# One input load held back behind TensorE's dummies, two head steps exchanged, one dummy pair less

## The chip, the cores and the metric

The kernel runs on one core of a Trainium2 chip. The metric is the device time of one execution in microseconds (us); lower is better.

## The reference

```python
x = A_x                                                # (1, 2048, 640) bf16
g = sigmoid((x * gate_w).sum(-1, keepdims=True))
# A: linear attention, 32 heads of 20
q, k, v = split(x @ wqkv)                              # wqkv (640, 1920)
pq, pk = q @ w_phi[h], k @ w_phi[h]                    # per head, 20 x 20
phi_q = concat(softmax(pq), softmax(-pq)); phi_k = concat(softmax(pk), softmax(-pk))
kv, z = phi_k^T v, sum_s phi_k
a = ((phi_q kv) / (phi_q z + 1e-6)) @ wo
# B: gated FFN, width 1728
b = (silu(x @ w_gate) * (x @ w_up)) @ w_down
return g * a + (1 - g) * b                             # bf16
```

## The kernel before

The 2048 tokens are cut into 16 tiles of 128 (and into 4 blocks of 512 for the FFN); the 640 columns of x into 5 chunks of 128. All work of all five engines is written as one list of steps. Two strings hold it: `LOADS` (L33), the transfers into the chip, and `ORDER` (L38), the compute steps. L759 goes through both and calls a function per word; every engine then has its instructions in that order. A tracker adds the semaphore waits that the reads and writes need. A DMA has a semaphore of its own; TensorE, ScalarE, VectorE and POOL have one each, which counts their tracked steps.

**Loads.** `LOADS` begins `x0 w0 x1 w1 x2 w2 x3 w3 w4 f0 h k0 k1 t4`. `x0` to `x3` (`load_x`, L369) bring the first four token tiles, 128 x 640, as they are, into `xs`. `w0` to `w4` (`load_wv`) bring the v columns of wqkv in chunks of 128 rows, into `wvg`. Two queues issue them: SP (SyncE) takes x0, w0, w1, w2, w3, and ScalarE takes x1, x2, x3, w4 (L361, L362). Ahead of x1 ScalarE's queue has the load of gate_w (`gwr`), and behind w4 the load of w_phi (`h`, tile `wph`), which waits for w3. Then follow on SP's queue the first FFN weights (`f0`), the transposed chunks of the k weights (`k`, tile `wT`), the token tiles 4 to 15 transposed by DMA (`t`), the q weights (`q`) and the rest.

**The head of the compute.** Words of `ORDER`:

- `H` (`warm`, L470): a dummy pair, two 128-column matmuls of constant ones, whose result nobody reads. The pair counts as one on TensorE's semaphore.
- `G`: gate_w is transposed into a column of `wvg`.
- `X0` to `X3` (`xpose`, L457): TensorE transposes the five chunks of a token tile (L308), VectorE copies them into `xT`; for tiles 0 to 2 the first chunk is copied apart from the other four.
- `U t.c` (`vpart`, L498): the two matmuls (320 and 321 columns, L296) of token tile t with chunk c of `wvg`. Five such parts make the v of a tile; then ScalarE copies it out. A tile's PSUM pair is held from its first part to its last.
- `V t`: the same for a later tile at once.

Before, the head runs `H0 ... H6 G H7 H8 X0 H9 H10 U0.0 X1 H11 U1.0 U0.1 X2 ...`.

**The rest.** `M` and `R` multiply w_phi into the k and q weights, with masked blocks of w_phi (`wbd`) that `Y` makes. `K`, `S`, `P` make phi_k, `E` adds up kv in PSUM banks 6 and 7. `N` (`kv_end`, L744) ends this: it has a loop of `NPEW` waits of TensorE on its own semaphore for the value 1, and then calls `kv_finish`, in which VectorE reads kv and z out of PSUM. `Z` transposes z (`zh`). Then come the q tiles (`Q`, `A`, `B`, `C`, `c`), the FFN (`F`), the attention output (`O`) and the down projection with the store (`D`).

PSUM is used as four pairs of banks. `next_pair` gives the pair used longest ago that isn't held; `H`, `G`, `X`, the first `U` of a tile and most other steps take one, so that the number and the order of the head's steps decide which pair a later step gets. Between `I` and `N` the fourth pair is left to kv.

Of the kernel before, what the change touches and what calls it, by code (L numbers as in the profile page):

```python
# [16 lines left out]
NV = 6  # L17
NWARM = 2
NWAIT = 6
NPEW = 32  # L20
FP = 120 * NCH
FK = FP + 8
ACTF = mybir.ActivationFunctionType
# [12 lines left out]
"""  # L36

ORDER = """  # L38
H0 H1 H2 H3 H4 H5 H6 G H7 H8 X0 H9 H10 U0.0 X1 H11 U1.0 U0.1 X2 U1.1 U2.0 U0.2 U1.2 U2.1
X3 U2.2 U0.3 U1.3 U2.3 U0.4 U1.4 U2.4 V3 Y F0.1 M1 i3 M0 F0.0 M2 V4 M3 M4 K0 K1 I S0 V6 V5 S1 P0  # L40
K3 K2 P1 E0 V9 K4 E1 S3 V7 P3 K5 S2 V8 V10 S4 P2 P4 E2 R0 E3 K6 S5 P5 S6 i4 E4 V14 K7 K8 P6 V15 S7
R2 E5 K9 S8 P7 R1 E6 K10 S9 V12 P8 E7 P9 K11 S10 P10 F0.2 R3 F1.2 E8 E9 K12 E10 S11 S12 K14 S14
# [11 lines left out]
class _Tracker:  # L54
# [90 lines left out]
    def run(self, eng, fn, reads=(), writes=(), dma=False):  # L145
        rkeys = list(dict.fromkeys(k for a in reads for k in self.keys_of(a)))
        wkeys = list(dict.fromkeys(k for a in writes for k in self.keys_of(a)))
        need = {}

        def req(ev, raw):  # L150
            if ev is None:
                return
            s, v = ev
            if s == eng and not dma and (eng == "pe" or not raw):
                return
            if v > need.get(s, 0):
                need[s] = v

        for k in rkeys:
            for kk in self._conflicts(k):  # L160
                req(self.lastw[kk], True)
                if k[0] == "psum":
                    for s, v in self.readers[kk].items():
                        req((s, v), False)
        for k in wkeys:
            for kk in self._conflicts(k):
                req(self.lastw[kk], True)
                for s, v in self.readers[kk].items():
                    req((s, v), False)
        self._wait(eng, need)  # L170
        ins = fn()
        if dma:
            sn = "d%d" % self.ndma
            self.ndma += 1
            self._add_sem(sn)
            inc = 16
        else:
            sn, inc = eng, 1
        ins.then_inc(self.sem[sn], inc)
        self.cnt[sn] += inc  # L180
        v = self.cnt[sn]
        snap = dict(self.known[eng])
        if not dma:
            snap[sn] = max(snap.get(sn, 0), v)
        self.evknow.setdefault(sn, {})[v] = snap
        ev = (sn, v)
        for k in wkeys:
            self.lastw[k] = ev
            self.readers[k] = {}
        for k in rkeys:  # L190
            r = self.readers[k]
            if r.get(sn, 0) < v:
                r[sn] = v
        return ev


def _build(nc, A_x, A_wqkv, A_w_phi, A_wo, B_x, B_w_gate, B_w_up, B_w_down, gate_w, out):
    tr = _Tracker(nc)
    pe, act, dve, pool, sp = nc.tensor, nc.scalar, nc.vector, nc.gpsimd, nc.sync
# [144 lines left out]
    def dma(e, dst, src, transpose=False):  # L344
        eo = tr.eng[e]

        def fn():
            if transpose:
                return eo.dma_start_transpose(dst, src)
            return eo.dma_start(dst, src)  # L350
        rd = [src] if src.tensor.name in tr.base else []
        wr = [dst] if dst.tensor.name in tr.base else []
        return run(e, fn, rd, wr, dma=True)
# [13 lines left out]
        return dma(e, dst, A_wqkv[c * P:(c + 1) * P, c0:c0 + D])  # L367

    def load_x(t):  # L369
        dma(XQ[t], xs[:, t, :], x2[t * P:(t + 1) * P, :])  # L370

    def load_xt(t):
# [27 lines left out]
    H0 = [0, 6, 12, 19, 25]  # L400
    H1 = [7, 13, 20, 26, 32]
# [342 lines left out]
    def kv_end():  # L744
        for _ in range(NPEW):
            pe.wait_ge(tr.sem["pe"], 1)
        kv_finish()
        ring["n"] = 4

    ops = {  # L750
        "H": lambda i: warm(), "i": fills, "X": xpose, "G": gcol, "U": vpart, "V": vtile,
        "M": lambda m: premult(1, m), "R": lambda m: premult(0, m),
        "K": ktile, "S": knorm, "P": kmul, "p": lambda t: kmul(t, "dve"), "E": kvtile, "x": load_x, "t": load_xt, "w": load_wv, "h": load_phi, "k": lambda m: load_wt(1, m), "q": lambda m: load_wt(0, m),
        "f": lambda i: load_ffn(FCUT[i], FCUT[i + 1]), "L": load_late_weights, "T": tail_weights, "J": gates,
        "Y": w_blocks, "I": kv_begin, "N": kv_end, "Z": z_row,
# [50 lines left out]
```

The softmax here doesn't subtract the row's maximum and nothing guards it: scores larger than these inputs give would overflow.

## Time and profile before

| what | value |
|---|---|
| median of 5 runs | 289.34 us (288.52 to 290.21) |
| the profiled execution's own time | 290.64 us |
| its span, first to last instruction | 289.4 us |
| TensorE (PE) busy, share of the span | 285.8 us, 99% |
| ScalarE (ACT) | 151.9 us, 52% |
| VectorE (DVE) | 163.5 us, 57% |
| POOL | 159.9 us, 55% |
| HBM read and written | 9.29 MB and 2.62 MB, 41 GB/s over the span |

PE is TensorE's matmuls, PEld its weight loads, which run beside them. SPq and ACTq are the instructions by which SyncE and ScalarE issue a DMA. The chain follows the work that ended last back to its beginning, at each step to what released it. A wait is idle time of an engine, put down to what came last. Spans on POOL are rough, and the ends of matmuls are modelled: their starts are the surer reading.

### The profile page before, as it was taken

The page shows a single profiled execution, that of the slowest core. Times are in us where ns is not written, and L with a number is a line of the kernel's source. Part 1 is how long each engine was busy: PE and PEld are TensorE (multiplying, and loading weights), DVE is VectorE, ACT ScalarE, POOL GpSimd, SP SyncE. Part 2 cuts the span into 40 slices and gives each one's busy share as a digit, 9 for nine tenths or more (in the row PEclk, how much of TensorE's full clock was granted, in tenths as well). Part 3 has the DMA queues.
Part 4 walks back from the last instruction along what each step waited for, and adds up shares of the span by engine and source line. Part 5 has one row for each costly group of instructions (what it writes and reads, how often), then busy time and mean ns, then how long its engine had stood idle before and what let it go on. Part 6 is the DMA issues. An engine that isn't in the chain of part 4 may idle for free.

```text
span 289.4 us, 4960 instructions
## 1 busy us (share of the span) xinstructions
PE 285.8 (99%) x1973; PEld 175.5 (61%) x1973; DVE 163.5 (57%) x243; ACT 151.9 (52%) x252; POOL 159.9 (55%) x125
## 2 busy tenths in 40 slices
PE   7999999999999999999999999999999999999997
PEld 6667777575644455557775546675554446656776
DVE  2245857587369978769992375980317899100000
ACT  0567768766685565584344763224676552234112
POOL 8275899979645798845633347450653658601000
DMA  7976797000010496402282102052020005210101
GB/s 220 194 119 129 108 280 274 3 0 3 0 49 0 70 329 124 83 17 47 53 144 73 28 1 50 2 120 70 2 50 0 2 2 116 58 45 0 49 23 48
DMA packets 48944, 21.62 MB, mean 75 GB/s; under 512 B 39384, under 2 KB 48792, under 8 KB 48920
## 3 DMA queue, kind: packets, MB, share of 16 engines
q1 hardware_dynamic: 47534, 20.59, 30.8%
q10 hardware_dynamic: 1386, 0.71, 0.9%
q8 instruction: 16, 0.26, 0.4%
q14 instruction: 8, 0.07, 0.1%
HBM read 9.29 MB, written 2.62 MB: 41 GB/s over the span
## 4 chain that ended last, share of the span: by engine, by line
PE 98%; DMA 1%; SPq 0%; DVE 0%; issue 0%
PE ps L296 97%; DMA wvg<-in_A_wqkv_dram 1%; PE ps L308 0%; SPq L350 0%; DVE osb L732 0%; PE ps L477 0%
## 5 line engine op out<-in xcount | busy, mean ns | idle before, releaser
L324 POOL TENSOR_TENSOR hT<-hT,us 128x512 bf16<-128x512 bf16 (+1 forms) x56 | 65.1, 1174 | 66.9 <-DVE hT L328 47.0
L328 DVE SCALAR_TENSOR_TENSOR hT<-hT,ps 128x512 bf16<-128x512 bf16 (+1 forms) x56 | 37.3, 682 | 68.6 <-ACT hT L314 55.0
L296 PE MATMUL ps<-xT,wg 128*128 128x512 bf16 x260 | 64.6, 379 | 0.0
L296 PE MATMUL ps<-xT,wu 128*128 128x512 bf16 x260 | 64.6, 379 | 0.0
L296 PE MATMUL ps<-wd,hT 128*128 128x320 bf16 (+2 forms) x462 | 63.9, 295 | 0.0
L324 POOL TENSOR_TENSOR ph<-eq,qc 128x1320 bf16<-128x1320 bf16 x16 | 42.4, 2647 | 25.6 <-DVE qc L637 20.8
L296 PEld LDWEIGHTS ps<-wd,hT 128*128 128x128 bf16 x462 | 44.5, 98 | 17.4
L296 PE MATMUL ps<-wqk,xT 128*128 128x320 bf16 x320 | 47.7, 299 | 0.0
L314 ACT ACTIVATE hT<-ps 128x512 bf16<-128x512 f32 (+2 forms) x60 | 35.7, 596 | 16.7 <-PE ps L296 16.5
L296 PEld LDWEIGHTS ps<-xT,wu 128*128 128x128 bf16 x260 | 25.4, 98 | 30.7
L314 ACT ACTIVATE us<-ps 128x512 bf16<-128x512 f32 (+1 forms) x56 | 33.5, 598 | 19.2 <-PE ps L296 18.2
L314 ACT ACTIVATE osb<-ps,omg 128x640 bf16<-128x640 f32 (+2 forms) x17 | 12.9, 758 | 55.7 <-PE ps L296 55.7
L296 PEld LDWEIGHTS ps<-xT,wg 128*128 128x128 bf16 x260 | 25.0, 98 | 27.8 <-ACT oT L314 0.8
L324 POOL TENSOR_TENSOR ekr<-ekr,krec 128x1280 bf16<-128x1280 bf16 x16 | 37.4, 2358 | 5.8 <-DVE krec L338 5.8
L296 PEld LDWEIGHTS ps<-wqk,xT 128*128 128x128 bf16 x320 | 30.5, 98 | 13.1 <-issue 0.4
L314 ACT ACTIVATE eq<-ps 128x640 bf16<-128x640 f32 x32 | 22.4, 704 | 20.9 <-POOL ph L324 10.7
L335 DVE TENSOR_REDUCE ksum<-ekr 128x64 f32<-128x1280 bf16 x16 | 23.5, 1470 | 11.8 <-ACT ekr L314 11.8
L314 ACT ACTIVATE ekr<-ps 128x640 bf16<-128x640 f32 x32 | 22.3, 704 | 8.7 <-PE ps L296 8.2
L296 PE MATMUL ps<-wvg,xT 128*128 128x320 bf16 (+1 forms) x160 | 25.6, 309 | 0.8 <-DMA wvg<-in_A_wqkv_dram 0.8
L335 DVE TENSOR_REDUCE qz<-eq 128x64 f32<-128x1280 bf16 x16 | 23.7, 1478 | 2.6 <-ACT eq L314 2.6
L296 PE MATMUL ps<-wog,oT 128*128 128x320 bf16 (+2 forms) x165 | 24.7, 294 | 0.0
L335 DVE TENSOR_REDUCE qw<-ez 128x64 f32<-128x1280 bf16 x16 | 23.6, 1476 | 0.0
(73 smaller groups left out, 191.1 us busy)
## 6 DMA issues: line engine op xcount, KB each, us to landing
out_dram<-osb SPq DMA_DIRECT2D x15, 160.0 KB, 2.0
wd<-in_B_w_down_dram SPq DMA_DIRECT2D x1, 2080.0 KB, 10.9
wg<-in_B_w_gate_dram SPq DMA_DIRECT2D x1, 1040.0 KB, 10.3
wu<-in_B_w_up_dram SPq DMA_DIRECT2D x1, 1040.0 KB, 12.3
wg<-in_B_w_gate_dram SPq DMA_DIRECT2D x1, 800.0 KB, 5.8
wu<-in_B_w_up_dram SPq DMA_DIRECT2D x1, 800.0 KB, 8.0
wog<-in_A_wo_dram SPq DMA_DIRECT2D x2, 375.0 KB, 7.3
wvg<-in_A_wqkv_dram SPq DMA_DIRECT2D x4, 160.0 KB, 3.9
```

The lines of the kernel that those rows point to most:

```text
L296: last = pe.matmul(o, lhsT=l, rhs=r, start=st, stop=sp_, skip_group_check=sk)
L314: return run("act", lambda: act.activation(o, i, func, scale=scale), rd, [o])
L324: return run(e, lambda: eo.tensor_tensor(o, a, b, op), [a, b], [o])
L328: return run("dve", lambda: dve.scalar_tensor_tensor(out=o, in0=a, scalar=s, in1=b, op0=op0, op1=op1), rd, [o])
L335: return run("dve", lambda: dve.tensor_reduce(o, i, AX.X, ALU.add), [i], [o])
```

## The change

Three edits and a constant.

- `load_x(1)` makes ScalarE wait for the value 4 of TensorE's semaphore before it issues the load of x1. At that point of the program only dummy pairs count, so this is the end of H3. The queue is in order: x2, x3, w4 and wph are issued after x1.
- In `ORDER` the dummy pair H10 stands behind U0.0 instead of in front of it; H11, which stood between X1 and the v parts, is gone; and U0.1 comes ahead of U1.0.
- `NPEW` goes from 32 to 40.

```diff
-NPEW = 32
+NPEW = 40
...
 ORDER = """
-H0 H1 H2 H3 H4 H5 H6 G H7 H8 X0 H9 H10 U0.0 X1 H11 U1.0 U0.1 X2 U1.1 U2.0 U0.2 U1.2 U2.1
+H0 H1 H2 H3 H4 H5 H6 G H7 H8 X0 H9 U0.0 H10 X1 U0.1 U1.0 X2 U1.1 U2.0 U0.2 U1.2 U2.1
...
     def load_x(t):
+        if t == 1:
+            act.wait_ge(tr.sem["pe"], 4)
         dma(XQ[t], xs[:, t, :], x2[t * P:(t + 1) * P, :])
```

## The prediction

> **What bounds the kernel now.** I read the page first (busy shares, then the chain that ended last), then the chain in order of time, and then only the first 10 us, because everything else is closed. The page says:
>
> ```profile
> PE 285.8 (99%) x1973; PEld 175.5 (61%) x1973; DVE 163.5 (57%) x243; ACT 151.9 (52%) x252; POOL 159.9 (55%) x125
> PE 98%; DMA 1%; SPq 0%; DVE 0%; issue 0%
> ```
>
> TensorE is busy 99% of the span and is 98% of the chain. The chain in order of time shows where the other 2% lies:
>
> ```profile
> 1.27 3.64 DMA wvg<-in_A_wqkv_dram
> 4.91 0.14 issue
> 5.04 0.69 PE ps L296 x2
> 5.74 0.53 PE ps L308 x5
> 6.27 0.21 PE ps L477 x2
> 6.48 1.07 PE ps L296 x4
> 7.55 0.53 PE ps L308 x5
> ```
>
> From 5.04 us on the chain never leaves TensorE. So the end moves only with the moment at which the dense stretch starts, and with the rate of its first matmuls. It starts when the first wv rows (w0) land, at 1.27 + 3.64 = 4.91. The waits say the same, and the table of 0.4 us stretches shows TensorE empty while the DMA engines are full:
>
> ```profile
> PE ps L296 <- DMA wvg<-in_A_wqkv_dram: 0.8, 1, 0.8
> 4.20:4.60 0.40, 0.01 (x1) 0.00 (x0) 0.04 (x1) 0.00 (x0) 0.40 (x2) 1.00 0.90 314
> 4.60:5.00 0.40, 0.00 (x0) 0.00 (x0) 0.00 (x0) 0.00 (x0) 0.40 (x2) 1.00 1.05 365
> ```
>
> (Columns: stretch, PE, PEld, DVE, ACT, POOL busy, clock, DMA share, GB/s.) What competes is in the timeline of the two issuing queues:
>
> ```profile
> 0.80 0.40 SPq L350 DMA_DIRECT2D xs<-in_A_x_dram  x1
> 1.27 1.85 SPq L350 DMA_DIRECT2D wvg<-in_A_wqkv_dram  x4
> 1.40 1.32 ACTq L350 DMA_DIRECT2D xs<-in_A_x_dram  x3
> 2.75 0.45 ACTq L350 DMA_DIRECT2D wvg<-in_A_wqkv_dram  x1
> 7.74 0.42 ACTq L350 DMA_DIRECT2D wph<-in_A_w_phi_dram  x1
> ```
>
> The issue times and landings of the single transfers in the trace give: x0 3.02, w0 4.91, x1 (issued 1.40) 5.09, w1 5.41, x2 5.81, w2 6.24, x3 7.30, w3 7.72, w4 8.07.
>
> Single matmuls give the rate. Starts of 320-column matmuls are 267 ns apart until 8.7 us and 138 ns apart after 8.9; the 128-column ones are 107 ns apart early and 55 late. The page's granted clock says 1.00 throughout and doesn't show this.
>
> [...]ten of w0's sixteen completions were in by 3.73, the last, [...]came at 4.91.[...]
>
> **The change, part by part.**
>
> *The wait.* TensorE's semaphore counts 1 per dummy pair and reaches 4 at 1.87 in the trace. A DMA that carries a wait left 0.02 us after its event (wph at 7.74, after w3 landed at 7.72), so x1 is issued at 1.89 instead of 1.40: +0.49. Behind it on ScalarE's queue stand x2, x3, w4 (each +0.49: 2.29, 2.76, 3.24), and wph, which waits for w3 of SP's queue and stays at 7.74. ScalarE's table load (8.25) and first copy (11.55) stay too. SP's and POOL's queues have no wait added.
>
> *Who wants these loads.* x1 landed at 5.09 and was used at 5.53, so it is tight. x2 (5.81, used 7.35), x3 (7.30, used 9.70) and w4 (8.07, used 11.08) keep 1.0 us or more after +0.49. Every later load up to 40 us has 2.9 us or more of slack in the trace, except wph, whose products are done at 13.29 and used at 15.22.
>
> *w0.* x1's first packets were on the DMA engines at 2.92, and should now be there at about 3.41, when SP's queue had begun 234 row packets, against 256 in x0 and w0 together, even with x1 beside them. So w0 should land sooner. Bounds: 3.73 (ten engines of sixteen) and 4.91 (unchanged, if one slow engine held it, not x1). I take 4.1. The issue step was 0.14, so the first matmuls with w0 (U0.0) start at 4.24, end at 4.24 + 2 x 0.267 = 4.77, and the dummy pair H10 behind them ends at 4.98.
>
> *x1.* Bounds: 5.09 (the bandwidth that w0 no longer shares pays for the delay) and 5.58 (+0.49 in full); beyond that, 6.2 if it meets a slow packet (single packets in this stretch took up to 0.68 us). I take 5.3, so X1 starts at 5.35: TensorE idles 0.37 there.
>
> *Order and dummies.* From X1 to X2 the trace of before has 5 transposes (0.53), H11 (0.21) and four matmuls (1.07): 5.53 + 1.81 = 7.35. After, H11 is gone and U0.1 covers VectorE's copy of x1 (0.23) that H11 covered: 5.35 + 0.53 + 1.07 = 6.95. The same count with w0 unchanged: 5.04 + 0.53 + 0.21 + 0.53 + 1.07 = 7.39, so the pair removed saves nothing by itself (H10 now stands behind w0 in its place, and before w0 TensorE idles anyway). U0.1 needs w1, at 5.41 before and wanted at 5.88: no wait. X2 is 0.39 earlier; all matmuls behind it are the same, and PSUM pairs are only renamed (the seven reuses whose predecessor differs all have their reader done over 1 us before).
>
> *At which rate.* If the clock switches at 8.8 as before, the 0.39 us gained are half-rate time, worth 0.20; if the switch moves along, 0.39. I take 0.3.
>
> *The eight waits more at L745.* They pass at once. 32 of them are 16 sequencer instructions, 0.106 us apart from 76.95 to 78.57, while the array works off queued matmuls until 79.38. Twenty end at 79.0, before the transpose of zh that follows them loads its weights at 79.24: nothing, with 0.2 us of cover left. If that cover is gone, the price is at most 4 x 0.106 = 0.42; below nothing I see no mechanism. They also replace the four TensorE instructions of the dummy pair[...].
>
> **Sum.** -0.3 us. The profiled execution took 290.64 (span 289.4 and 1.24 around), 1.30 above the median of 289.34; its own time would be 290.3, the median 289.0. A change within 0.5% (1.45 us) is about what a measurement of this kernel can't tell from none.
>
> **Rivals.**
>
> *An earlier clock.* The idle of 0.84 us before w0 shrinks[...] For it: the five times spread over 1.69 us[...]. Against it: a gap of about 0.4 us in front of X1 stays, and one before w0.
>
> *Nothing.* One slow engine, not x1, held w0: X2 at 7.39, time 289.4. For it: one packet at 4.05 took 0.61 us.
>
> *x1 becomes the bound (slower).* In front of X1, TensorE waits for x1 instead of w0. The point is X1 at 7.35 - 1.60 = 5.74, x1 landing at 5.70. At 6.2 the loss is 0.5 us: 289.8.[...] For it: x1, x2 and x3 all leave 0.49 later on a saturated DMA. Against it: the same bytes in the same total time, and w0 served first.
>
> *The wait does nothing.* It can't: the fourth pair ends 0.46 us after x1's old issue.
>
> **How the numbers follow.** Forecast, a small gain (0 to 1.4 us): 0.56. Earlier clock, past 1.45 us: 0.12. Nothing: 0.12. x1 late by less than 1.45 us: 0.12[...]. So faster 0.12, same 0.80, slower 0.08. The likeliest time is 289.0. Its head runs from 288.7 (x1 at 5.09: X2 0.60 earlier) to 289.8 (x1 at 6.2); a median of few runs that spread 1.69 adds some 0.5 each side, and part of the earlier clock belongs in: 287.6 to 290.2.
>
> **What would show it.** Right: x1's issue at 1.9; w0 landing before 4.5; the wait in front of TensorE's first wv matmuls shorter than 0.8 and a new one of TensorE for x1 in front of its transposes; X2 near 6.95; no idle later, none near 79 us. Wrong: w0 still at 4.9, x1 after 5.7[...].

## The result, and the profile after

The changed kernel takes 290.55 us (median of 36 executions, 288.87 to 291.77); the kernel before, beside it, 289.23 (71 executions). The ratio is 1.0033, 95% interval 1.0021 to 1.0046: slower by about a third of a percent, where 289.0 us was forecast and 287.6 to 290.2 stated. (One slow run, 293.43 us in a_nowait below, is left out of its ratio; medians and counts include it.)

The medians hide the shape. Half of the executions after (18 of 36) lie above 290.7 us; before it was 8 of 71, and 14 of 227 over all runs of the kernel before in this study. The change made a rare outcome common. The line at 290.7 is a rough one: the execution profiled before, at 290.64, belongs to the upper group by its trace, as shown below. Drawn at 290.5, the counts are again 18 of 36 after, and 10 of 71 before.

The profiled execution after is one of the other half: its own time is 289.37, its span 288.1, less than the 289.4 of the execution profiled before. One profile against one profile points the wrong way here.

The chain in order of time, after (start, length, what):

```profile
0.84 1.24 PE ps L479 x10
2.08 0.17 ACTq L350
2.25 0.03 issue
2.28 4.43 DMA xs<-in_A_x_dram
6.71 0.05 issue
6.76 0.45 PE ps L308 x5
7.21 1.37 PE ps L296 x10
8.58 0.28 PE ps L308 x5
8.86 69.40 PE ps L296 x640
```

The transfer in the chain is no longer w0 but x2, issued by ScalarE's queue at 2.28 and landed at 6.71; and the chain reaches back through that queue to TensorE's dummies, which release it. The last two lines are X3 and what follows it. The timeline of ScalarE's issues shows the hold (x1 leaves at 1.89 instead of 1.40), and TensorE's timeline where it waits:

```profile
1.89 1.32 ACTq L350 DMA_DIRECT2D xs<-in_A_x_dram  x3
3.24 0.45 ACTq L350 DMA_DIRECT2D wvg<-in_A_wqkv_dram  x1
4.08 0.69 PE L296 MATMUL ps<-wvg,xT 128*128 128x320 bf16 x2 [0.19 <-DMA wvg<-in_A_wqkv_dram]
4.57 0.42 PE L479 MATMUL ps<-const-bfloat16-1.0 128*128 128x128 bf16 x2
5.22 0.45 PE L308 MATMUL ps<-ident,xs 128*128 128x128 bf16 x5 [0.23 <-DMA xs<-in_A_x_dram]
5.51 0.71 PE L296 MATMUL ps<-wvg,xT 128*128 128x320 bf16 x4
6.76 0.45 PE L308 MATMUL ps<-ident,xs 128*128 128x128 bf16 x5 [0.55 <-DMA xs<-in_A_x_dram]
7.05 1.53 PE L296 MATMUL ps<-wvg,xT 128*128 128x320 bf16 x10
8.42 0.44 PE L308 MATMUL ps<-ident,xs 128*128 128x128 bf16 x5
```

w0 is early and its wait is down to 0.19 us. Two new waits stand in its place, in front of X1 (5.22) and of X2 (6.76). The bracket counts from the modelled end of the matmul before; from start to start the gaps are 0.54 and 0.84 us. The rate is the other thing to read. The granted clock in the tables is 1.00 in both profiles, so "half" and "full" clock stand here for the spacing of the matmuls' starts alone: 267 and 138 ns with 320 columns, 107 and 55 with 128. The five transposes of X1 take 0.71 us at half rate (a_npew32 and d_gap below); here they take 0.45. In this execution the dummy pair at 4.57 is still 107 ns apart, and from 5.28 the transposes are 56 apart: the clock was full at 5.3 us, while before it was half until 8.7. That is why this profile is short.

One number puts everything else aside. The span less the start of X3 is 279.7 us after (288.12 - 8.42) and before (289.40 - 9.70), and, within 0.06 us, in all profiles of this study but one (c_pe2, with one stall of 0.34 at 13.5 us). So in the profiled executions the differences arise before X3, from two things: when the loads of the head land (x1, x2 and the first chunks of w), and when the clock goes full.

### The profile page after: what moved, and what is told of

Its sections match the earlier page's. It is cut to its first block, busy times and chain, and to the rows that moved or that the text cites. A ratio compares the mean times of both kernels' runs of the same rounds, so it can differ in the third digit from the quotient of the medians.

```text
span 288.1 us, 4960 instructions
## 1 busy us (share of the span) xinstructions
PE 284.4 (99%) x1971; PEld 173.9 (60%) x1971; DVE 163.5 (57%) x243; ACT 151.8 (53%) x252; POOL 159.8 (55%) x125
## 4 chain that ended last, share of the span: by engine, by line
PE 97%; DMA 2%; DVE 0%; ACTq 0%; issue 0%
PE ps L296 97%; DMA xs<-in_A_x_dram 2%; PE ps L479 0%; PE ps L308 0%; DVE osb L734 0%; ACTq L350 0%
## 5 line engine op out<-in xcount | busy, mean ns | idle before, releaser
L296 PE MATMUL ps<-wvg,xT 128*128 128x320 bf16 (+1 forms) x160 | 24.5, 301 | 0.2 <-DMA wvg<-in_A_wqkv_dram 0.2
## 6 DMA issues: line engine op xcount, KB each, us to landing
wg<-in_B_w_gate_dram SPq DMA_DIRECT2D x1, 1040.0 KB, 10.1
```

The costliest lines, as they stand in the source:

```text
L296: last = pe.matmul(o, lhsT=l, rhs=r, start=st, stop=sp_, skip_group_check=sk)
```

## The experiments

Theory 1: the wait makes x1 and x2 late and TensorE idles for them. Theory 2: idle time in the head, from wherever, makes the clock go full later in more executions. Theory 3: the waits at NPEW, or a wait as such, cost. The expectations of the first two runs have theory 2 in a narrower form (fewer dummies ahead of w0 make the idle time, and the wait matters little); both runs refute that form, and the later ones try the wider one. In every profile below, "late clock" means that the last half-rate matmul starts after 8.4 us.

**a_nowait: the changed kernel without its wait.**

```diff
-        if t == 1:
-            act.wait_ge(tr.sem["pe"], 4)
```

> The changed kernel without the wait: x1 leaves at 1.40 us again, order, dummies and NPEW stay changed. Theory 1 (the wait delays x1 and x2, TensorE idles for them): the loss is gone, 288.9 to 289.4 us, x2 lands near 5.8 instead of 6.7. Theory 2 ([...]so the full clock comes later in more executions; the wait matters little): 290.2 to 290.6, as with the wait. Theory 3 (the waits at NPEW cost): 290 or more too.

Measured: 289.34 us, ratio to the kernel before 1.0004 (0.9989 to 1.0020); 3 of 22 above 290.7. w0 landed at 4.00, x1 at 4.30, x2 at 5.53. The loss is the wait, as theory 1 said; order, dummies and NPEW together make no difference that can be seen.

**b_wait: the wait alone, in the kernel before.**

```diff
     def load_x(t):
+        if t == 1:
+            act.wait_ge(tr.sem["pe"], 4)
```

> The kernel before with the wait alone; order, dummies and NPEW as before. Theory 1: 290.2 to 290.6, x2 again near 6.7 and TensorE idle in front of X1 or X2. Theory 2: 289.2 to 289.6, since three dummy pairs stand where they stood and w0 comes sooner. Theory 3: 289.2.

Measured: 291.10 us, 1.0049 (1.0028 to 1.0069); 11 of 15 above 290.7. In the profile w0 landed at 3.48, w1 at 5.91 and x1 only at 6.09; X1 started at 6.13 and the clock was late. The wait needs none of the other edits to cost, and it costs more than the 290.2 to 290.6 of theory 1.

**a_npew32: the changed kernel with NPEW back.**

```diff
-NPEW = 40
+NPEW = 32
```

> The changed kernel with NPEW = 32 again, nothing else. Theories 1 and 2: 290.3 to 290.8, no change against the changed kernel, and no idle of TensorE near 78 us in either. Theory 3 (four instructions of waits, 0.42 us at most[...]): 289.9 or less.

Measured: 290.90 us, 1.0037 (1.0011 to 1.0062); 7 of 10 above 290.7. The interval holds the changed kernel's 1.0033. TensorE is dense at the place of these waits in both. The profile is worth more than the time: it caught the late-clock case of the same head. TensorE's timeline there:

```profile
3.95 0.71 PE L296 MATMUL ps<-wvg,xT 128*128 128x320 bf16 x2
4.46 0.42 PE L479 MATMUL ps<-const-bfloat16-1.0 128*128 128x128 bf16 x2
6.43 0.71 PE L308 MATMUL ps<-ident,xs 128*128 128x128 bf16 x5 [1.56 <-DMA xs<-in_A_x_dram]
6.94 1.28 PE L296 MATMUL ps<-wvg,xT 128*128 128x320 bf16 x4
8.01 0.74 PE L308 MATMUL ps<-ident,xs 128*128 128x128 bf16 x5
8.54 2.30 PE L296 MATMUL ps<-wvg,xT 128*128 128x320 bf16 x10
10.68 0.44 PE L308 MATMUL ps<-ident,xs 128*128 128x128 bf16 x5
```

x1 landed at 6.38, TensorE idled from 4.67 to 6.43, and X1, X2 and the v parts up to 10.1 ran at half rate. X3 starts at 10.68, 2.26 after the profile of the changed kernel; the spans differ by the same 2.26 (290.38 - 288.12).

**a_fill4: four dummy pairs where TensorE waits for x1.**

```diff
-X0 H9 U0.0 H10 X1 U0.1 U1.0 X2
+X0 H9 U0.0 H10 H11 H12 H13 H14 X1 U0.1 U1.0 X2
...
-NPEW = 40
+NPEW = 8
```

> The changed kernel with four more dummy pairs (0.85 us at half clock) between H10 and X1, where TensorE waits for x1, and NPEW = 8 so that TensorE's instructions stay as many. Theory 2: the late-clock executions become rare, the slow cluster (290.7 to 291.8) thins from half of the executions to under a fifth, median 289.2 to 289.7, the last half-rate matmul before 6 us in the profile. Theory 1: no gain; the pairs delay X1 by up to 0.6 us where x1 is there already, 290.6 to 291.0.

Measured: 289.69 us, 1.0017 (1.0003 to 1.0032); 1 of 22 above 290.7, against 18 of 36. Work that computes nothing wins back 0.86 of the 1.32 us in the medians, and about half of the loss by the ratios, whose intervals overlap; the count is the clear part (drawn at 290.5, 3 of 22). Theory 1 alone, with no gain and 290.6 to 291.0, falls. The loads stay late (x1 6.00, x2 7.81 in the profile):

```profile
3.82 0.49 PE L296 MATMUL ps<-wvg,xT 128*128 128x320 bf16 x2
4.14 0.75 PE L479 MATMUL ps<-const-bfloat16-1.0 128*128 128x128 bf16 x10
6.04 0.45 PE L308 MATMUL ps<-ident,xs 128*128 128x128 bf16 x5 [1.16 <-DMA xs<-in_A_x_dram]
6.33 0.71 PE L296 MATMUL ps<-wvg,xT 128*128 128x320 bf16 x4
7.85 0.45 PE L308 MATMUL ps<-ident,xs 128*128 128x128 bf16 x5 [0.81 <-DMA xs<-in_A_x_dram]
```

The five pairs run at full rate (their starts are some 59 ns apart), and so does all that follows; TensorE then only waits for data. But the clock was full before the added pairs began: the second matmul of U0.0 starts at 4.00, and the next start is 138 ns later. So this profile doesn't show the pairs at work; that they thin the upper group rests on the count. (NPEW = 8 by itself was not tried; from 40 to 32, in a_npew32, nothing changed.) It does show what late data can cost with the clock full: its own time is 290.45, because X2 waits for x2.

**d_gap: idle time put in by hand, no load moved.**

```diff
-        if t == 1:
-            act.wait_ge(tr.sem["pe"], 4)
...
     def xpose(t):
+        if t == 1:
+            tr._wait("pe", dict([wv_evs[1]]))
```

> The changed kernel without the wait on ScalarE's queue; instead TensorE waits in front of X1 until w1 has landed (5.3 us or later), so that the idle time in front of X1 is put in by hand and no load moves. Clock theory: a third or more of the executions are above 290.7 us, median 289.6 to 291. If only the late data count (x2 is in time here): one cluster, X1 and what follows at most 0.6 us later, 289.3 to 289.8, nothing above 290.7 but a few.

Measured: 290.19 us, 1.0025 (1.0008 to 1.0042); 9 of 22 above 290.7. x1 landed at 4.36, but X1 had to wait for w1 (6.60):

```profile
6.65 0.71 PE L308 MATMUL ps<-ident,xs 128*128 128x128 bf16 x5 [1.72 <-DMA wvg<-in_A_wqkv_dram]
7.16 1.28 PE L296 MATMUL ps<-wvg,xT 128*128 128x320 bf16 x4
8.23 0.74 PE L308 MATMUL ps<-ident,xs 128*128 128x128 bf16 x5
8.76 1.83 PE L296 MATMUL ps<-wvg,xT 128*128 128x320 bf16 x10
```

That is more than a third, as the clock theory had it; late data alone was to leave no more than a few above 290.7. A gap in front of X1 is enough to bring the upper executions, though no load was held; the one that was profiled has the late clock. This and a_fill4 are the two sides of theory 2: put the idle in, and the upper group comes; fill it, and it nearly goes.

**c_bfill3: the gap of the kernel before, filled.**

```diff
-X0 H9 H10 U0.0 X1 H11 U1.0 U0.1 X2
+X0 H9 H10 H12 H13 H14 U0.0 X1 H11 U1.0 U0.1 X2
...
-NPEW = 32
+NPEW = 8
```

> The kernel before with three more dummy pairs (0.64 us at half clock) in front of U0.0, where TensorE waits for w0, and NPEW = 8 so that TensorE's instructions stay as many. Clock theory: the executions above 290.2 us (a sixth of the kernel before) vanish, median 288.8 to 289.3. If the idle time plays no part in the clock: same spread as before, 289.2 to 289.6.

Measured: 289.44 us, 1.0003 (0.9986 to 1.0020); none of 14 above 289.91. The upper executions are missing, as expected, though 14 are few to show the absence of something seen 14 times in 227. The median gained nothing (288.8 to 289.3 was expected). In the profile w0 landed at 3.89, and the pairs held U0.0 back to 4.69; w1 landed at 6.68 and TensorE waited for it at full rate. With the clock up early, the next landing is the bound here.

**The delay in steps: d_pe1, c_pe2, d_pe3, d_pe6.** Only the value of the wait differs from the changed kernel:

```diff
-            act.wait_ge(tr.sem["pe"], 4)
+            act.wait_ge(tr.sem["pe"], 1)      # d_pe1; 2, 3 and 6 in the others
```

> The changed kernel with the wait for the value 1, which TensorE reaches at 1.23 us, before x1's old issue at 1.40: a wait that delays nothing. If what the wait costs is the delay: 289.0 to 289.5 us, like the changed kernel without a wait. If a wait on this queue costs by itself: 289.8 or more, as the value 2 gave (289.95).

> The changed kernel with the wait for the value 2 (about 1.44 us) instead of 4: x1 leaves at 1.46, 0.06 later than without a wait. Pairing theory (what counts is beside which w transfer x1 is served): x1 still lands with w0, some 0.2 us after it, before w1; 289.1 to 289.6 us. If a wait on this queue costs by itself, or every tenth of a microsecond counts: 289.8 or more.

> The changed kernel with the wait for the value 3 (1.65 us; x1 leaves near 1.67, 0.27 later than without). Step theory (x1 either catches the first round of transfers beside w0 or comes with the second): either 289.2 to 289.6 with x1 landing before 5.1, or 290.3 to 290.9 with x1 after 5.1. Graded theory (every tenth of a microsecond costs): 290.0 to 290.4.

> The changed kernel with the wait for the value 6 (2.29 us; x1 leaves near 2.31, 0.42 later than in the changed kernel). Step theory: x1 still comes with the second round, landing 5.3 to 6.5, and the time hardly moves against the changed kernel: 290.5 to 291.0. Graded theory: x1 0.4 later, 290.9 to 291.5.

| kernel | x1 issued | x1 landed | median us | ratio (95%) | above 290.7 |
|---|---|---|---|---|---|
| a_nowait | 1.40 | 4.30 | 289.34 | 1.0004 (0.9989 to 1.0020) | 3 of 22 |
| d_pe1 | 1.40 | 4.33 | 289.62 | 1.0014 (1.0001 to 1.0027) | 2 of 22 |
| c_pe2 | 1.46 | 4.98 | 289.95 | 1.0023 (1.0000 to 1.0046) | 8 of 22 |
| d_pe3 | 1.68 | 5.73 | 290.93 | 1.0060 (1.0045 to 1.0076) | 4 of 8 |
| changed kernel | 1.89 | 5.17 | 290.55 | 1.0033 (1.0021 to 1.0046) | 18 of 36 |
| d_pe6 | 2.32 | 6.07 | 291.75 | 1.0085 (1.0061 to 1.0109) | 5 of 6 |

(Issue and landing are of the one profiled execution.) A wait that delays nothing (d_pe1) costs 0.3% at most, and leaves the upper group as rare as in the kernel before; theory 3 may hold a part of the loss, but not the executions above 290.7. The pairing and step theories (x1 is on time if it is served beside w0, late if it is served beside w1, and nothing lies between) fail: 0.06 us of delay already gives 8 of 22, though x1 landed ahead of w1, and 0.42 beyond the changed kernel costs on, more than even the graded theory had (290.9 to 291.5). The time grows with the delay, though not evenly: d_pe3 stands above the changed kernel, with only eight executions.

**c_x1sp: x1 on SP's queue behind w0, the wait moved to x2.**

```diff
-    XQ = ["sp", "act", "act", "act"]
+    XQ = ["sp", "sp", "act", "act"]
...
-        if t == 1:
+        if t == 2:
```

> The changed kernel with x1 on SP's queue behind w0 and the wait moved to x2, which now heads ScalarE's loads (x1 leaves near 1.7, w1 near 2.2, x2 at 1.89). Pairing theory: w0 lands alone near 3.5 to 4.0, x1 next near 4.0 to 4.6, w1 with x2 after 5.2; TensorE's wait in front of X1 is under 0.3 us, so the full clock comes early: 288.5 to 289.2. If x1 is late because any load issued after w0 is slow to arrive on loaded DMA engines: x1 past 5.2 again, 290 or more.

Measured: 291.19 us, 1.0063 (1.0033 to 1.0093); 8 of 12 above 290.7. w0 landed at 3.60 and x1 at 5.67, though its issue was at 1.73 and nothing held it. So the hope that x1 would follow 0.5 us behind w0 was wrong, and x1 can be late without ScalarE's queue.

**c_w1hold: w1 held too.**

```diff
     def load_wv(c):
+        if c == 1:
+            sp.wait_ge(tr.sem["pe"], 6)
```

> The changed kernel with SP's queue held in front of w1 until the sixth dummy pair (w1 leaves at 2.31 instead of 1.72; w2, w3 and the rest follow). Pairing theory: x1 is no longer served beside w1 and lands before it, by 4.6; TensorE's idle in front of X1 falls under 0.3 us, but w1 (5.2 to 6) can bound the next part; 288.9 to 289.9. If x1's own later issue is all there is: x1 at 5.2 to 6.4 as before, 290.3 to 290.8.

Measured: 290.00 us, 1.0023 (1.0006 to 1.0041); 8 of 22 above 290.7. x1 landed at 4.99, a microsecond ahead of w1 (6.01). That is sooner than in any profile with x1 at 1.89 and w1 at 1.72, but not by the 4.6 that was expected, and TensorE waited in front of X1 (0.50 start to start), for w1 (0.79) and for w2 (0.35): in this execution the gain at one place came back as waits at the next.

## Why the prediction was wrong, point by point

Two terms carry the miss: x1's landing, taken as 5.3 and 5.9 in the mean of four profiles, and what comes with it, a full clock that is late in many executions (half lie above 290.7, and all four profiled executions above that line, in other runs, have it late), where all that is slower by more than 0.5% had a chance of 0.08. Both were worked out from one profile of before that was not a usual one.

**What bounds the kernel: right.** TensorE's chain, and the head alone. Nothing after X3 moved by as much as 0.1 us in thirteen of fourteen profiles.

**NPEW, the order, the pair removed: right.** No gap near 78 us; a_nowait is 1.0004, and a_npew32 agrees with the changed kernel.

**w0: right in direction and value, wrong in worth.** It was to land at 4.1 and landed at 3.95; with x1 held at 1.89 and SP's order unchanged the four profiles have 3.95, 3.81, 3.48 and 3.56. But the yardstick was bad. The step took 4.91 from the one profile of before as what w0 costs; without a hold it landed at 4.00, 3.89, 3.89 and 3.88 in a_nowait, c_bfill3, d_pe1 and d_gap. The profiled execution of before was an unusual one, 290.64 us against a median of 289.34, which I had noted and put down to nothing. The usual gain was some 0.2 us, not 0.8.

**x1: the term that was mis-sized.** "Bounds: 5.09 and 5.58 ... I take 5.3." The same four profiles with the hold have 5.17, 6.38, 6.09 and 6.00 (mean 5.9); without it x1 lands at 4.30, 4.25, 4.33 and 4.36 (mean 4.3), and at 5.09 only in the profile of before. A delay of 0.49 us in the issue became 1.6 us in the landing, 1.4 if that profile is counted in. Half of it is a tail: a landing is the last of a transfer's sixteen completions (w0's tenth in the profile of before was in at 3.73 and its sixteenth at 4.91, and the matmul that waited for it started at 5.04). The tenth of x1's comes at 4.10 to 4.16 without the hold, in the profile of before too, and at 4.68 to 5.23 with it; the last comes 0.1 to 0.2 us after the tenth without (0.93 in the profile of before), and 0.5 to 1.35 after it with the hold. My step held that "the bandwidth that w0 no longer shares pays for the delay", on DMA engines that I took as full, because their share was 1.0. The table of 0.5 us stretches, for a_nowait (first four lines) and a_npew32 (the other four), shows part of what happened; the last two columns are DMA share and GB/s:

```profile
2.50:3.00 0.50, 0.50 (x5) 0.36 (x5) 0.18 (x1) 0.00 (x0) 0.43 (x4) 1.00 0.90 218
3.00:3.50 0.50, 0.50 (x6) 0.35 (x5) 0.02 (x1) 0.00 (x0) 0.42 (x3) 1.00 0.91 302
3.50:4.00 0.50, 0.50 (x6) 0.31 (x3) 0.30 (x2) 0.00 (x0) 0.38 (x3) 1.00 1.01 300
4.00:4.50 0.50, 0.45 (x3) 0.28 (x3) 0.33 (x1) 0.00 (x0) 0.50 (x1) 1.00 0.90 325
```

```profile
2.50:3.00 0.50, 0.50 (x5) 0.37 (x5) 0.18 (x1) 0.00 (x0) 0.43 (x4) 1.00 0.88 307
3.00:3.50 0.50, 0.46 (x6) 0.31 (x5) 0.00 (x0) 0.00 (x0) 0.42 (x3) 1.00 0.94 164
3.50:4.00 0.50, 0.50 (x7) 0.44 (x6) 0.28 (x2) 0.00 (x0) 0.38 (x3) 1.00 0.92 233
4.00:4.50 0.50, 0.50 (x5) 0.27 (x4) 0.37 (x1) 0.00 (x0) 0.50 (x1) 1.00 0.88 228
```

The share is near 1 in both, the bytes are not: from 3.0 to 4.5 us (302 + 300 + 325) x 0.5 = 464 KB against (164 + 233 + 228) x 0.5 = 313 KB. Of the missing 151 KB some 126 are on ScalarE's queue, which carries x1, and SP's transfers don't make them up (191 KB against 209). It is not a plain loss, though: half a microsecond earlier the order is the other way, from 1.5 to 4.5 us a_npew32 is 102 KB behind, and to 6.5 us only 33. The bytes come later, and x1's with them. In a_npew32 some packets of SP's queue that begin between 3.18 and 3.22 take 0.31 to 1.40 us, where most take 0.055, which lets a share be full without bytes. Such packets are not peculiar to the hold: six of a_nowait's that begin between 2.58 and 2.79 take 0.33 to 0.54, and in the profile of before, from 2.5 to 3.0, a share of 0.90 went with 133 GB/s. Then x1 lands right behind w1 (0.18 us after in a_npew32 and b_wait, 0.21 in a_fill4), as if the two were served together, where before it landed right behind w0 (0.18 us after in the profile of before, 0.30 in a_nowait). c_w1hold, where x1 lands at 4.99 with w1 held back, fits; d_pe3, where x1 lands at 5.73 ahead of w1, doesn't. Why x1 is late is not shown: no run tries the slow packets, or the order of service, by itself.

**x2: wrong.** "x2 ... keep 1.0 us or more" was reckoned from a wanted time of 7.35, at half rate. It landed at 6.71 to 7.81 with the hold, and at full rate it is wanted at 6.05 (the last v matmul in front of X2 starts at 5.92 after). So in the profiled execution after, of the better half, x2 is the bound: 0.84 us of gap. The clock was full and X2 waited for x2 in a_fill4 too, and in both the own time is x2's landing plus 282.6 to 282.7 us (289.37 - 6.71 and 290.45 - 7.81).

**The clock: the case was there, its chance wasn't.** The rival "x1 becomes the bound" gave the point (x1 landing at 5.70); that the gap there can also make the full clock late was my estimate, which the trace of before didn't show. Three of the four profiles with the hold have x1 past 5.70; the clock is late in two of them, and in a_fill4 it was full before x1 came. Of the fourteen profiles the five with a late clock have own times of 290.64 to 291.62, the nine others 289.19 to 290.45. What failed is the weight: 0.08 for all that is slower by more than 0.5%, because "the same bytes in the same total time". The share of executions above 290.7 went from 6% (14 of 227; 11% in the 71 beside the changed kernel) to 50%, and that moves the median by most of the gap between the clusters. The base was wrong as well. The profile of before, at half rate until 8.7, is itself one with a late clock; the profiles a_nowait and d_pe1, whose loads leave as before, go full at about 6.5 and 6.8. So for the usual execution the rival "an earlier clock" had little left to win, and a later one had much to cost (the five late profiles, 290.64 to 291.62). One kernel has both outcomes from execution to execution, and a change of the head acts on how often: in a_nowait, c_pe2 and the changed kernel most executions lie near 289 to 290.4 or 290.7 to 292, and 3 of 22, 8 of 22 and 18 of 36 lie above 290.7. What decides between the two in one execution no run shows, and the size isn't fixed: c_pe2 reaches 292.89, and five of d_pe6's six executions lie from 291.44 to 293.08.

**The sum.** Of +1.32 us in the median, 0.86 go when idle time is filled (a_fill4), which speaks for the clock; the rest, about 0.5, is by difference what the late x1 and x2 cost themselves. The sizes are rough: with 18 executions on either side, the median after lies in the empty stretch between 290.36 and 290.75. In the means the loss is 0.96 us, and 0.54 stay with a_fill4. The forecast had -0.3, from a w0 gain of 0.8 that is 0.2 and an x1 loss of 0.2 that is 1.6 (times of landing, of which not all reaches the end). A loss of a third of a percent could be told from none after all: the interval of the ratio is 0.25% wide, half of the 0.5% that the prediction took as out of reach.

**Still open.** Why c_pe2 (0.06 us of delay) is above d_pe1 so clearly in its share of executions above 290.7 (8 of 22 against 2 of 22); what makes the clock go full when it does; why x1's last completions are so late; and why d_pe3 is above the changed kernel. The distance from the dense start to the full rate isn't fixed: it was 3.7 us in the profile of before (5.04 and about 8.8), in d_gap 2.8 us (6.65 and about 9.4), in b_wait 3.0 us (6.13 and 9.1). No version here beats the kernel before.

## What to carry to other kernels

Where one engine is busy 99% of the time, look for what is left in its ramp: count every new wait in the first microseconds twice, once for its length and once for the clock that it may delay (in d_gap, with the wait put in by hand, 9 of 22 executions lay above 290.7 against 3 of 22 in a_nowait, and the profiled one was at half rate until 9.0). Dummies in such a wait thinned the upper executions here (1 of 22 in a_fill4 against 18 of 36), but they gained the median of the kernel before nothing (c_bfill3). Before reckoning from a landing time in the head, look at several executions, above all where the profiled one's own time is off the median; and read DMA bytes, not the DMA share, before calling the engines full (here 0.94 went with 164 GB/s and 0.91 with 302). A load held back to let another through didn't pay here: w0 gained some 0.2 us and x1 lost 1.6.

## What the runs showed of the hardware that I had not expected

- A transfer issued 0.49 us later landed 1.6 us later (5.9 against 4.3, means of four profiles each; the profile of before, with 5.09, is not in them), and one on the other queue behind w0 (c_x1sp) was no sooner: 5.67.
- Ten dummy matmuls after w0 in a_fill4 ran 59 ns apart: the clock was full from 4.0 us, 3.2 us after TensorE's first matmul at 0.84, with gaps between. In d_gap it was half until 9.0.
- The DMA share stayed at 0.94 with 164 GB/s (a_npew32, 3.0 to 3.5 us), where 0.91 went with 302 (a_nowait, the same stretch) and 0.90 with 133 (before, 2.5 to 3.0).
